# Two heads on separate 64-row halves of TensorE in both score passes of a segment-wise attention block

## The chip, the cores and the metric

The kernel runs on one core of one Trainium2 chip. The metric is the device time of one execution in microseconds (us), and lower is better. The kernel before takes 1942.58 us, the median of three runs (1942.33, 1942.58 and 1944.91).

## The reference

`block` computes one transformer block on 2048 tokens of width 576: a modulated layer norm, an attention with 32 heads of 18 features, a second modulated layer norm and a gated feed-forward of width 4608. The attention works on four segments of 512 tokens. Inside a segment it is an ordinary causal softmax, and a running memory of earlier segments is added. Cut to the part that the change touches:

```python
for s in range(4):
    qs, ks, vs = q[:, :, s], k[:, :, s], v[:, :, s]
    logits = einsum("bhqd,bhkd->bhqk", qs, ks) * scale + mask
    p = softmax(logits, axis=-1)
    a_dot = einsum("bhqk,bhkd->bhqd", p, vs)
    o = g * (phi(qs) @ M) / (phi(qs) @ z) + (1 - g) * a_dot
    M, z = M + phi(ks).T @ vs, z + phi(ks).sum()
```

Everything is float32. To keep enough digits, q and k are split into a high and a low part of TensorE's fp32r type, so that one head's dot product of 18 features becomes one of 54 rows (high by high, high by low, low by high).

## The kernel before

The kernel has three stages. Stage one (up to about 258 us) normalises, projects q, k and v (line 93, tiles `pp` and `pv`) and builds the memory matrices. Its order is made by a scheduler. Stage two (258 to about 617 us) is the attention of all heads. Its order is written out by hand. Stage three is the feed-forward (lines 1090 and 1152), which the change does not touch.

**Units.** The attention is cut into 32 units: a segment and a group of four heads. For each unit `load_stack` (L151) brings k and q into two stacks, `kst` and `qst`. Two heads, called e = 0 and e = 1, form a pair, and a unit has two pairs, a = 0 and a = 1. In `kst` a pair's heads lie one below the other: rows 0 to 53 hold e = 0, rows 54 to 107 hold e = 1. In `qst` each of the four heads has its own column block with its 54 rows filled and the other head's 54 rows zero (L117, L118 write the zeros once for each of the stack buffers). A product over all 108 rows therefore gives one head's scores, because the zero rows cancel the other head.

**First pass** (`p1_step`, L164): queries stand still and keys stream. Its only purpose is each query's largest score. It has four steps i = 3, 2, 1, 0 with n = 512, 384, 256, 128 keys. TensorE writes the scores into a PSUM bank (tag `s1`, two buffers), and VectorE adds the mask and takes the maximum (L179, tile `junk`). The maxima go through GpSimd, a transpose (L193, `pmt`), a ScalarE copy and a DMA to `mD`, and `load_m` (L160) brings them back as two further rows, 108 and 109, of `qst`. Rows 108 and 109 of `kst` are ones (L119).

**Second pass** (`p2_step`, L565): keys stand still and queries stream, over 110 rows, so that the maximum is subtracted inside the product. Its steps are j = 0 to 3 with n = 512, 384, 256, 128 queries. TensorE writes into a bank with tag `s2` (two buffers), ScalarE takes the exponential (L579, tile `Pt`) and GpSimd zeroes the upper triangle (L583). For n up to 256 one product streams two heads, and one exponential takes 512 columns.

**Order.** The loop at L1168 runs unit u's second pass beside unit u+2's first pass. Each is a generator that yields after each PSUM bank: four banks for n = 512, four for n = 384, two for n = 256, one for n = 128, eleven in all. In each of the eleven steps the loop issues one bank of the second pass, one bank of the first pass, and then the events that the string `PAT[...][k]` lists. Events with TensorE work are `V` (L596, probabilities by values, four heads on four 32-column tiles of the array), `m` (the transpose of the maxima), `c` (L617, transposes of the result), `A` (L765, the memory's part), `R` and `Z` (transposes of a finished segment) and `M` (L694, the output projection of the segment before, from unit 9 on). The event `n` sends the maxima out and issues `load_m`. Engines take their instructions in the order in which they were issued, so a product that waits for a bank holds up what stands behind it on TensorE.

The first passes of units 0 and 1 lie in stage one (`early`, L243), a bank at a time between the projections.

## Time and profile before

| what | value |
|---|---|
| median of three runs | 1942.58 us |
| span of the profiled execution | 1946.8 us |
| TensorE busy over the span | 1901.2 us, 98% |
| VectorE busy | 1533.1 us, 79% |
| ScalarE busy | 824.8 us, 42% |
| GpSimd busy | 1020.6 us, 52% |
| granted TensorE clock, mean | 0.993 |
| first product of the second pass of unit 0 / unit 31 | 260.34 us / 609.05 us |

The profiled execution is one more execution, with the hardware profiler on. Its span is 4.2 us longer than the median of the runs. All durations come from it. A busy TensorE is not a TensorE at its peak: the record of a product holds its whole way through the array, and the next product starts before it ends. What a product costs in a stream is the distance from its start to the start of the next one. In such a listing a row is one or several equal instructions: start, length, engine, line, operation, output and inputs, shape and count. PEld is the load of the operand that stands still ("weights"), which can run while the product before is under way.

### The profile page before, as it was taken

Reading aid. Unit: us, or ns where it says so; the run is one execution under the profiler, and the core shown is the slowest. Engines: PE = TensorE matmul, PEld = TensorE weight load, DVE = VectorE, ACT = ScalarE, POOL = GpSimd, SP = SyncE. Lnnn points to the kernel's source line nnn. Section 1 sums busy time; section 2 is a strip of 40 time slices with the busy share of each in tenths; the row PEclk is TensorE's granted clock in tenths of the full one; section 3 lists DMA queues with packets and bytes.
Section 4 is the critical chain, followed back from the end, with each engine's and each line's share of the span. In section 5 each row is a group of like instructions: output and inputs, shape, how many; then the busy total and the mean of one; then the engine's idle time right before and its main releaser. Section 6 shows DMA issues by size and latency. Waiting matters only on the chain.

```text
span 1946.8 us, 31901 instructions
## 1 busy us (share of the span) xinstructions
PE 1901.2 (98%) x11119; PEld 1593.1 (82%) x11119; DVE 1533.1 (79%) x3218; ACT 824.8 (42%) x1652; POOL 1020.6 (52%) x1396
## 2 busy tenths in 40 slices
PE   7999999999999899999999999999999999999999
PEld 4887865676766678888888888888888888888888
DVE  6575257878786999898898988979888888878886
ACT  2222256767667434344344343433333333333332
POOL 5322235455544866556565565556565564655551
PEclk9999999999999899999999999999999999999999
DMA  7776564444443332232222222174211211112111
GB/s 207 244 227 233 203 204 140 131 139 150 136 128 125 92 135 101 89 106 80 80 106 83 82 84 78 60 264 146 74 62 45 74 62 59 60 62 74 62 57 50
DMA packets 114354, 223.59 MB, mean 115 GB/s; under 512 B 22992, under 2 KB 40784, under 8 KB 112720
## 3 DMA queue, kind: packets, MB, share of 16 engines
q1 hardware_dynamic: 111936, 215.61, 34.2%
q0 software_dynamic: 576, 5.11, 0.7%
q8 instruction: 88, 1.44, 0.3%
q10 hardware_dynamic: 1680, 0.82, 0.2%
q14 instruction: 74, 0.61, 0.1%
HBM read 161.11 MB, written 60.36 MB: 114 GB/s over the span
## 4 chain that ended last, share of the span: by engine, by line
PE 88%; DVE 4%; DMA 4%; ACT 1%; issue 1%; POOL 1%; SPq 1%; POOLq 0%; ACTq 0%; DVEq 0%
PE M L1090 39%; PE pd L1152 23%; PE pp L93 4%; PE s L576 4%; PE av L596 4%; PE s L174 4%; PE pv L93 3%; PE pw L694 2%; DMA O<-in_wgu_dram 1%; DMA mD<-mr 1%; PE pn L765 1%; PE pm L429 1%; PE px L617 1%; PE pr L346 1%; DVE y L923 1%
## 5 line engine op out<-in xcount | busy, mean ns | idle before, releaser
L1090 PE MATMUL M<-y,wh 128*128 128x512 f32 x2520 | 792.0, 393 | 5.0 <-DVE cu L1106 2.1
L1090 PEld LDWEIGHTS M<-y,wh 128*128 128x128 f32 x2520 | 473.7, 188 | 101.7 <-issue 3.9
L1067 POOL TENSOR_TENSOR wh<-O,wh 32x128 fp32r<-32x128 f32 x504 | 296.6, 593 | 423.0 <-ACT wh L1065 271.3
L1090 PE MATMUL M<-y,wl 128*128 128x512 f32 x1008 | 394.7, 392 | 0.0
L1059 POOL TENSOR_TENSOR O<-O 128x384 f32<-128x384 f32 x288 | 315.4, 1095 | 75.0 <-DMA O<-in_wgu_dram 42.9
L1152 PE MATMUL pd<-dh,ah 128*128 128x288 f32 x1152 | 340.3, 295 | 0.2 <-DVE acc L1155 0.2
L1152 PE MATMUL pd<-dl,ah 128*128 128x288 f32 x1152 | 340.3, 295 | 0.0
L1152 PE MATMUL pd<-dh,al 128*128 128x288 f32 x1152 | 340.1, 295 | 0.0
L1110 ACT CAST ah<-sg 128x512 fp32r<-128x512 f32 x144 | 89.5, 621 | 547.8 <-DVE sg L1107 422.0
L1155 DVE TENSOR_TENSOR acc<-acc,pd 128x576 f32<-128x576 f32 x288 | 216.5, 752 | 111.8 <-PE pd L1152 108.4
L1066 DVE TENSOR_TENSOR wl<-O,wh 128x256 fp32r<-128x256 f32 x504 | 286.2, 568 | 6.0 <-ACT wh L1065 5.2
L179 DVE CUSTOM_DVE_ANT_0 junk<-s,tri 128x256 bf16<-128x256 f32 (+3 forms) x512 | 228.7, 487 | 77.2 <-PE s L174 69.8
L1065 ACT CAST wh<-O 128x384 fp32r<-128x384 f32 x504 | 242.8, 507 | 0.0
L1152 PEld LDWEIGHTS pd<-dl,ah 128*128 128x128 f32 x1152 | 217.4, 189 | 11.8
L1152 PEld LDWEIGHTS pd<-dh,ah 128*128 128x128 f32 x1152 | 216.7, 188 | 11.6 <-DVE acc L1155 0.6
L579 ACT ACTIVATE Pt<-s 128x512 f32<-128x512 f32 (+1 forms) x352 | 186.5, 559 | 88.1 <-PE s L576 72.0
L1152 PEld LDWEIGHTS pd<-dh,al 128*128 128x128 f32 x1152 | 216.6, 188 | 0.0
L1090 PEld LDWEIGHTS M<-y,wl 128*128 128x128 f32 x1008 | 190.0, 188 | 29.6
L1102 ACT ACTIVATE sg<-sg 128x512 f32<-128x512 f32 x144 | 91.2, 633 | 222.7 <-DVE sg L1101 222.7
L576 PE MATMUL s<-qs,ks 110*128 110x512 f32 (+2 forms) x384 | 150.5, 409 | 5.7 <-DMA qs<-mD 4.4
L174 PE MATMUL s<-ks,qs 108*128 108x256 f32 (+3 forms) x512 | 141.2, 327 | 3.3 <-DMA ks<-kD 1.4
L583 POOL TENSOR_SCALAR_AFFINE_SELECT Pt<-Pt 128x512 f32<-128x512 f32 x128 | 81.6, 648 | 100.6 <-ACT Pt L579 100.2
(428 smaller groups left out, 2836.6 us busy)
## 6 DMA issues: line engine op xcount, KB each, us to landing
O<-in_wgu_dram SPq DMA_DIRECT2D x72, 768.0 KB
ks<-kD SPq DMA_DIRECT2D x68, 216.0 KB
qs<-qD SPq DMA_DIRECT2D x68, 216.0 KB
kD<-fh SPq DMA_DIRECT2D x16, 512.0 KB
qD<-fh SPq DMA_DIRECT2D x16, 512.0 KB
yD<-st SPq DMA_DIRECT2D x28, 256.0 KB
y<-yD SPq DMA_DIRECT2D x7, 1024.0 KB
wml<-in_w_mod_dram SPq DMA_DIRECT2D x24, 216.0 KB
```

The source lines that it names most:

```text
L93: nc.tensor.matmul(ps, lhsT=a, rhs=b, start=(k == 0), stop=(k == 13))
L174: nc.tensor.matmul(bank[:, n * (h - h0):n * (h - h0) + n], lhsT=qst[b][0:108, h, 128 * i:128 * i + 128], rhs=kst[b][0:108, h // 2, 0:n], s ...
L179: nc.vector.tensor_tensor_reduce(junk[:, :n], bank[:, n * (h - h0):n * (h - h0) + n], tri[:, L - n:], 1.0, -3e38, op0=ALU.add, op1=ALU.max ...
L576: nc.tensor.matmul(bank[:, n * (g - h):n * (g - h + w)].rearrange("p (a b) -> p a b", a=w), lhsT=kst[u % NB][0:110, g // 2, 128 * j:128 * ...
L579: nc.scalar.activation(pt[:, h:h + per, :n], bank[:, :n * per].rearrange("p (a b) -> p a b", a=per), AF.Exp, scale=SCALE)
L1059: nc.gpsimd.tensor_tensor(o[:, d], o[:, a], o[:, b], op=op)
L1065: nc.scalar.copy(wh, o)
L1066: later.append(lambda: nc.vector.tensor_tensor(wl, o[:, 0:2], f32(wh[:, 0:2]), op=ALU.subtract))
L1067: later.append(lambda: nc.gpsimd.tensor_tensor(wh[32:64, 2], o[32:64, 2], f32(wh[32:64, 2]), op=ALU.subtract))
L1090: nc.tensor.matmul(bank, lhsT=a, rhs=b, start=(n == 0), stop=(n == 6))
L1152: nc.tensor.matmul(pd[:, h, :288], lhsT=a[:, tk], rhs=w[:, f, sl], start=(k == 0), stop=(k == 5))
L1155: nc.vector.tensor_tensor(o, o, pd[:, :, :288], op=ALU.add)
```

## The change

Each head of a pair now has its own half of the array. Head e = 0 uses rows 0 to 53 (and 54, 55 for the maxima and ones), head e = 1 uses rows 64 to 117 (and 118, 119), in both stacks. `qst` shrinks from four column blocks to two, and the zeros and their memsets are gone. Each product is over 54 or 56 rows and is issued for a tile of 64 by 128 cells, at row 0 or row 64, where it was issued for the whole 128 by 128 array. In each step the second pass takes heads of one half and the first pass heads of the other half, and the next step swaps them. For n = 256 and n = 128 the two products of a bank are now the two heads with the same e. For n = 128 a unit has two banks where it had one, so both passes have twelve steps, and the event strings are spread over twelve. The rows of ones and the maxima are loaded by two DMAs where one did it.

```diff
     def new_stack(b, stk):
-        qst[b] = stk.tile([P, 4, L], F32R, tag=f"qs{b}", name=f"qs{b}")
+        qst[b] = stk.tile([P, 2, L], F32R, tag=f"qs{b}", name=f"qs{b}")
         kst[b] = stk.tile([P, 2, L], F32R, tag=f"ks{b}", name=f"ks{b}")
-        nc.vector.memset(f32(qst[b][:, 0:2]), 0.0)
-        nc.gpsimd.memset(f32(qst[b][:, 2:4]), 0.0)
-        nc.sync.dma_start(f32(kst[b][108:110]).rearrange("p a (b c) -> p (a b) c", c=P),
-                          ones[0:2, :].unsqueeze(1).to_broadcast([2, 8, P]))
+        for e in range(2):
+            nc.sync.dma_start(f32(kst[b][64 * e + 54:64 * e + 56]).rearrange("p a (b c) -> p (a b) c", c=P),
+                              ones[0:2, :].unsqueeze(1).to_broadcast([2, 8, P]))
...
     # p1_step
-        per = L // n if n <= 256 else 1
-        for h0 in range(0, 4, per):
+        groups = [((0, 1),), ((0, 0),), ((1, 1),), ((1, 0),)] if n > 256 else [((0, 1), (1, 1)), ((0, 0), (1, 0))]
+        for g, hs in enumerate(groups):
...
-                                 lhsT=qst[b][0:108, h, 128 * i:128 * i + 128],
-                                 rhs=kst[b][0:108, h // 2, 0:n], start=True, stop=True)
+                r = slice(64 * e, 64 * e + 54)
+                nc.tensor.matmul(bank[:, n * x:n * x + n], lhsT=qst[b][r, a, 128 * i:128 * i + 128],
+                                 rhs=kst[b][r, a, 0:n], start=True, stop=True)
...
     # p2_step
+        groups = [((0, 0),), ((0, 1),), ((1, 0),), ((1, 1),)] if n > 256 else [((0, 0), (1, 0)), ((0, 1), (1, 1))]
...
-                                 lhsT=kst[u % NB][0:110, g // 2, 128 * j:128 * j + 128],
-                                 rhs=qst[u % NB][0:110, g:g + w, 128 * j:L], start=True, stop=True)
+                r = slice(64 * e, 64 * e + 56)
+                nc.tensor.matmul(bank[:, n * x:n * x + n], lhsT=kst[u % NB][r, a, 128 * j:128 * j + 128],
+                                 rhs=qst[u % NB][r, a, 128 * j:L], start=True, stop=True)
...
-            for k in range(11):
+            for k in range(12):
```

34 lines of the change are left out of this document (17 added, 17 removed), and 6 rows, old and new, of the table PAT.

## The prediction

> **What bounds the kernel now.** I read the page first: the span and the chain of work that ended last.
>
> ```profile
> span 1946.8 us, 31901 instructions
> PE 88%; DVE 4%; DMA 4%; ACT 1%; issue 1%; POOL 1%; SPq 1%; POOLq 0%; ACTq 0%; DVEq 0%
> ```
>
> TensorE carries 88% of the chain, so shorter score passes can pay, if the stretches in which they lie are themselves held by TensorE. So next come the busy times by stage.
>
> ```profile
> 93.00:118.00 25.00, 24.11 (x114) 18.20 (x113) 23.93 (x68) 5.78 (x11) 5.74 (x9) 1.00 0.63 210
> 118.00:165.00 47.00, 47.00 (x300) 41.46 (x299) 28.76 (x71) 13.41 (x25) 10.72 (x16) 1.00 0.73 245
> 258.00:380.00 122.00, 113.70 (x778) 71.55 (x778) 92.93 (x383) 88.37 (x181) 63.17 (x114) 0.97 0.48 142
> 380.00:620.00 240.00, 239.58 (x1799) 166.91 (x1797) 183.93 (x770) 167.32 (x336) 118.83 (x246) 1.00 0.44 131
> ```
>
> Columns after the length: TensorE, its weight loads, VectorE, ScalarE, GpSimd, granted clock. The first passes of units 0 and 1 lie between 93 and 165 us: up to 118 us VectorE is as full (23.93 of 25) as TensorE, after that TensorE alone is. The attention has two parts. From 380 us (units 11 on) TensorE is never free (239.58 of 240) while VectorE has 77% and ScalarE 70%. Before 380 us TensorE has pauses (113.70 of 122), though neither VectorE nor ScalarE is fuller. The chain of waits says what fills them:
>
> ```profile
> 254.28 9.62 DMA qs<-qD
> 298.22 5.61 DMA mD<-mr
> 303.90 1.80 DMA qs<-mD
> ...
> 291.79 1.83 DMA qs<-mD
> ...
> 326.88 1.87 DMA qs<-mD
> ```
>
> The second is the round trip of a unit's maxima through DRAM: 5.61 + 1.80 = 7.4 us, and it ends when the next unit's second pass can begin. The last two rows are the ends of the same trip in two more units. In all of them a faster TensorE waits for the DMA.
>
> **What the change removes: every second score product's time.** The prices, start to start, are in the timeline of one unit; one product of 512 columns, of 384, of 256 and of 128 (with a weight load each):
>
> ```profile
> 589.78 0.50 PE L576 MATMUL s<-qs,ks 110*128 110x512 f32 x1
> 590.12 0.40 PE L174 MATMUL s<-ks,qs 108*128 108x512 f32 x1
> 590.35 0.40 PE L576 MATMUL s<-qs,ks 110*128 110x512 f32 x1
> 590.59 0.39 PE L174 MATMUL s<-ks,qs 108*128 108x512 f32 x1
> 590.90 0.42 PE L596 MATMUL av<-Pt,vq 128*32 128x256 f32 x4
> ...
> 594.78 0.34 PE L576 MATMUL s<-qs,ks 110*128 110x384 f32 x1
> 594.95 0.34 PE L174 MATMUL s<-ks,qs 108*128 108x384 f32 x1
> 595.13 0.34 PE L576 MATMUL s<-qs,ks 110*128 110x384 f32 x1
> ...
> 598.43 0.50 PE L576 MATMUL s<-qs,ks 110*128 110x512 f32 x1
> 598.77 0.40 PE L174 MATMUL s<-ks,qs 108*128 108x256 f32 x2
> 599.01 0.40 PE L576 MATMUL s<-qs,ks 110*128 110x256 f32 x2
> 599.25 0.56 PE L174 MATMUL s<-ks,qs 108*128 108x128 f32 x4
> ...
> 599.13 0.53 PEld L174 LDWEIGHTS s<-ks,qs 108*128 108x128 f32 x4
> ```
>
> A product of 512 takes 0.23 us (590.12, 590.35, 590.59), of 384 takes 0.175, of 256 takes 0.12 (two from 598.77 to 599.01). Four of 128 are set by their weights: four loads last 0.53, one 0.19 (the common length), so (0.53 - 0.19)/3 = 0.11 each.
>
> If the two halves work side by side, a step costs one half's products. Steps of 512: 0.46 becomes 0.23, four of them save 0.93. Steps of 384: 0.35 becomes 0.175, four save 0.70. Steps of 256: 0.23 + 2 x 0.12 = 0.47 becomes 0.24, two save 0.47. The one step of 128 (2 x 0.12 + 0.11 x 3 + 0.06, about 0.63) becomes two steps of 2 x 0.11, saving 0.19. That is 2.3 us for each unit with both passes, 30 of them: 69 us. Whether halves overlap is not in this trace. Its nearest row is the four column tiles of line 596:
>
> ```profile
> 597.44 1.07 PE L596 MATMUL av<-Pt,vq 128*32 128x512 f32 x8
> ...
> 589.00 0.16 PEld L596 LDWEIGHTS av<-Pt,vq 128*32 128x32 f32 x8
> ```
>
> Eight records of 512 columns are over after 598.43 - 597.44 = 0.99 us, four tiles at a time; one after another at 0.23 they would need 1.8. The eight weight loads of another such step are over in 0.16. I take full overlap, and keep none as the other end. The Trainium skill, "TensorE: Matmul & The Clock Gate", Part 3 (measured speedup), gives 3.07 times for four row tiles of 32 rows at 512 columns; no run here shows it, and by it the saving for two halves would also be nearly whole.
>
> **What it adds: changes of the array's tiling.** Stage one has one place where products for a 64-row tile stand among full ones.
>
> ```profile
> 53.35 0.40 PE L93 MATMUL pp<-hr,wqkh 128*128 128x512 f32 x1
> 53.58 0.40 PE L93 MATMUL pp<-hr,wqkl 128*128 128x512 f32 x1
> 53.91 0.46 PE L416 MATMUL ptk<-ident,pf 64*128 64x64 f32 x4
> 54.30 0.50 PE L93 MATMUL pp<-hh,wqkh 128*128 128x512 f32 x1
> 54.64 0.40 PE L93 MATMUL pp<-hh,wqkl 128*128 128x512 f32 x1
> ...
> L416 PE MATMUL ptk<-ident,pf x60: 222/272/421, 39.0 to 189.1; 128*128 128x128 f32 x48, 64*128 64x64 f32 x12
> ```
>
> Into the tile: 53.58 to 53.91 is 0.33 where 0.23 is usual, so 0.10. After such a change the weights can't be loaded ahead, as the first score product after line 596 shows (589.78 to 590.12, 0.34 instead of 0.23): 0.11 more. Out of it: the group's last product is 0.22 long, so it starts at 53.91 + 0.46 - 0.22 = 54.15, the next at 54.30, which is 0.15 where products this short stand 0.06 apart (0.24 for three distances, the first with 0.11 for weights): 0.09; and then again unloaded weights, 54.30 to 54.64, 0.11. So 0.20 in and 0.20 out.
>
> How often, I counted in the built programs' order of TensorE's instructions. Beside a `V` nothing is new, since line 596 (128x32 tiles) changes the tiling already before. New are the visits next to `M`, `c`, `A` and `R`. Units 0 to 8 (no `M` yet): 18 in, 17 out, 7 us. Units 9 to 31: 99 in, 93 out, 38 us. Stage one, where one bank of a first pass stands alone between projections and so has no partner: 22 and 22, 9 us.
>
> **How much of it reaches the end.** Units 9 to 31: 21 x 2.3 - 38 = 10 us less TensorE time; TensorE is full there, but the exponentials bound some steps:
>
> ```profile
> PEld s L576 <- ACT Pt L579: 37.2, 64, 0.8
> ```
>
> TensorE's weight loads wait 64 times for ScalarE to free a bank. I take 85%: 8.5 us faster. Units 0 to 8: 9 x 2.3 - 7 = 14 us less; the maxima's round trip does not shrink, only the steps before it, so I take 40%: 5.5 us faster (bounds 0 and 14). Stage one: half of the visits lie before 118 us, where VectorE hides part: 7 of 9 us slower. Then SP's queue at the start of the attention:
>
> ```profile
> 249.72 1.49 SPq L119 DMA_DIRECT2D ks<-ones  x2
> 254.28 0.90 SPq L158 DMA_DIRECT2D qs<-qD  x1
> ```
>
> Two DMAs of ones become four, 0.75 each, ahead of unit 2's loads, whose last (254.28, landing 9.62 later) ends the wait of the first score product of unit 2: 1.5 us slower, on the path. The second `load_m` DMA costs at most one more issue of a few tenths, only in the few units that wait for the maxima: under 1 us, I take 0. The dropped memsets (GpSimd, VectorE) run under the projections and give 0 (with that cover gone, a microsecond each). 32 more exponentials: two of 256 columns for one of 512 on an engine that is 30% free, 0. The shorter last step frees VectorE earlier, which `m` may use, 0.
>
> Sum: -8.5 - 5.5 + 7 + 1.5 = -5.5 us against the profiled span, 1946.8 to 1941.3. The median of the runs is 4.2 below that span, so I put the same difference there: 1942.6 - 5.5, about **1937 us**.
>
> **The rivals.**
>
> 1. *Slower: the halves don't really overlap.* Place: every step; price: the changes of tiling (7 + 38 + 9) and 1.5 stay, 55 us, against a saving that shrinks. With none of it, nine tenths of the 55 us show, as TensorE is not quite full everywhere: 1942.6 + 50 = 1993. It decides at 55/69: below four fifths of full overlap the kernel is slower. A halfway form: products overlap but the two halves' weights load one after the other, 0.11 each. Then steps of 384 save 0.53 in all, of 256 0.06, of 128 lose 0.25, and each of some eight entries per unit costs 0.11 more: 0.93 + 0.53 + 0.06 - 0.25 - 0.9 = 0.4 per unit, 12 us against 55, about 1981. Against both: line 596's four column tiles and their loads run side by side. For: no row of before has two row tiles at once. 10% and 14%.
> 2. *Products start strictly in the order of issue.* In a step of 256 or 128 a bank's two products share a half, and the partner's come behind, so only the middle two overlap: three slots of 0.12 or 0.11 instead of two. That takes 4 slots, 0.46 us, from each of 30 units, 14 us, some 11 at the end: 1948. The Trainium skill has this as a rule in "TensorE: Matmul & The Clock Gate", Part 3 (what overlaps and what doesn't). Line 596's rows do not show the issue order of its passes, so the trace leaves it open. 8%.
> 3. *The other engines set the pace.* The order was cut for eleven steps, VectorE needs 184 of 240 us in bursts, and the maxima's round trip ends more units. The saving stays small, the switches in stage one are whole: 1942.6 + 1.5 + 7 - 6, about 1945. For it: the 64 waits above. 13%.
> 4. *More than I take.* Both parts of the attention turn TensorE's relief into time, 10 + 14, and a tenth of the 45 us of tiling changes there hides behind the waits for banks: 1942.6 - 24 - 4.5 + 8.5, about 1922. For it: the 64 waits for banks, which are there already; against it: the maxima's round trip. 10%.
>
> **How the numbers follow.** My forecast, 1928 to 1946, has 45%. The range leaves out the case without overlap and the far end of the fourth: 1918 to 1985. A measurement of this kernel can tell about 0.2%, 3.9 us, from no change: 1938.7 to 1946.5 is "same". Faster: most of the forecast (34%) and the fourth rival, 44%. Same: 10% of the forecast, 6% of the third, 2% of the second, 18%. Slower: the first rival's 24%, 6% of the second, 7% of the third, and 1% left, 38%.
>
> **What would show it.** Right: in the timeline of a unit, a product of L576's successor and the first pass's product start within hundredths of each other, 0.11 + 0.23 later the next; entries and exits of 0.2; units after 380 us shorter by about 0.4; stage one longer by 7. Wrong: partners 0.23 apart (first rival), weight loads of partners 0.11 apart (its halfway form), partners of 256 waiting for the second of the bank before (second), TensorE pauses ended by VectorE or ScalarE (third).

## The result and the profile after

The changed kernel takes **1974.26 us** (median of four runs, 1971.58 to 1975.89), the kernel before beside it 1942.45 us. The ratio is 1.0156, with a 95% interval of 1.0142 to 1.0171: 1.6% slower. The forecast was 1937, faster. The time lies inside the range of 1918 to 1985, but the likeliest case and its sign were wrong.

The page of the changed kernel, first its span, then the chain of work that ended last by engine:

```profile
span 1974.2 us, 32222 instructions
PE 88%; DMA 4%; DVE 4%; ACT 2%; issue 1%; SPq 1%; POOL 1%; DVEq 0%; ACTq 0%; POOLq 0%
```

The chain says nothing new: TensorE carries 88% as before. What moved is seen by stage. The attention is cut at the first product of units 0, 9 and 31 in each kernel. The columns after the length are TensorE, its weight loads, VectorE, ScalarE, GpSimd (busy us and count), then the granted clock, the share of DMA and GB/s. First the kernel before (units 0 to 8, units 9 to 30):

```profile
260.30:359.80 99.50, 91.20 (x614) 55.13 (x612) 76.70 (x319) 72.32 (x149) 54.15 (x97) 0.97 0.49 146
359.80:609.00 249.20, 249.15 (x1858) 174.32 (x1854) 197.86 (x827) 175.31 (x353) 122.77 (x255) 1.00 0.43 130
```

Then the changed kernel:

```profile
268.30:381.00 112.70, 102.52 (x649) 51.91 (x649) 76.87 (x317) 74.63 (x156) 53.94 (x97) 0.76 0.44 128
381.00:637.20 256.20, 252.44 (x1946) 146.55 (x1944) 198.79 (x830) 178.66 (x375) 123.82 (x255) 1.00 0.44 128
```

Three places lose. Stage one ends at 268.3 instead of 260.3 (+8). Units 0 to 8 take 112.7 instead of 99.5 (+13), and their clock column reads 0.76 instead of 0.97: TensorE ran at half clock for about half of that time. Units 9 to 30 take 256.2 instead of 249.2 (+7) at an undisturbed clock. The rest gives back 0.8, and the sum is the 27.4 us between the two spans. The medians are 31.8 apart, because the profiled execution of the kernel before was 4.4 us longer than its median run and that of the changed kernel was not; so some 4 us of the loss are in no row here.

Yet the overlap is there. This is the end of one unit and the start of the next (unit 24) in the changed kernel, TensorE only; each row is start, length, engine, line:

```profile
556.48 0.39 PE L578 MATMUL s<-qs,ks 56*128 56x256 f32 x1
556.49 0.38 PE L175 MATMUL s<-ks,qs 54*128 54x256 f32 x1
556.71 0.28 PE L578 MATMUL s<-qs,ks 56*128 56x256 f32 x1
556.71 0.28 PE L175 MATMUL s<-ks,qs 54*128 54x256 f32 x1
...
560.29 0.64 PE L598 MATMUL av<-Pt,vq 128*32 128x256 f32 x8
560.86 0.50 PE L578 MATMUL s<-qs,ks 56*128 56x512 f32 x1
560.86 0.50 PE L175 MATMUL s<-ks,qs 54*128 54x512 f32 x1
561.29 0.43 PE L598 MATMUL av<-Pt,vq 128*32 128x128 f32 x8
561.65 0.28 PE L194 MATMUL pmt<-ident,mc 128*32 128x128 f32 x1
561.86 0.50 PE L578 MATMUL s<-qs,ks 56*128 56x512 f32 x1
```

Partners start within 0.01 us. A step of 512 between two V events (560.86 to 561.29) takes 0.43. The same steps before:

```profile
534.16 0.50 PE L576 MATMUL s<-qs,ks 110*128 110x512 f32 x1
...
535.28 0.64 PE L596 MATMUL av<-Pt,vq 128*32 128x256 f32 x8
535.86 0.50 PE L576 MATMUL s<-qs,ks 110*128 110x512 f32 x1
536.20 0.40 PE L174 MATMUL s<-ks,qs 108*128 108x512 f32 x1
536.53 0.43 PE L596 MATMUL av<-Pt,vq 128*32 128x128 f32 x8
536.88 0.28 PE L193 MATMUL pmt<-ident,mc 128*32 128x128 f32 x1
536.92 0.48 PE L576 MATMUL s<-qs,ks 110*128 110x512 f32 x1
```

There the step takes 536.53 - 535.86 = 0.67. So 0.24 is saved on it, where 0.23 was priced. Note the last two rows of both fences too: from the small transpose `pmt` to the next score product it was 0.04, now it is 0.21.

### The profile page after: what moved, and what is told of

Read it like the earlier page. It is cut to its first block, busy times and chain, and to the rows that moved or that the text cites. A ratio compares the mean times of both kernels' runs of the same rounds, so it can differ in the third digit from the quotient of the medians.

```text
span 1974.2 us, 32222 instructions
## 1 busy us (share of the span) xinstructions
PE 1922.1 (97%) x11247; PEld 1559.8 (79%) x11247; DVE 1521.0 (77%) x3214; ACT 830.9 (42%) x1684; POOL 1015.4 (51%) x1392
## 4 chain that ended last, share of the span: by engine, by line
PE 88%; DMA 4%; DVE 4%; ACT 2%; issue 1%; SPq 1%; POOL 1%; DVEq 0%; ACTq 0%; POOLq 0%
PE M L1092 40%; PE pd L1154 23%; PE s L578 5%; PE pp L93 5%; PE av L598 4%; PE pw L696 3%; PE pv L93 2%; PE s L175 2%; DMA mD<-mr 1%; DVE y L925 1%; PE pm L430 1%; PE px L619 1%; ACT Pt L581 1%; PE pn L767 1%; DMA qs<-mD 1%
## 5 line engine op out<-in xcount | busy, mean ns | idle before, releaser
L1068 DVE TENSOR_TENSOR wl<-O,wh 128x256 fp32r<-128x256 f32 x504 | 274.7, 546 | 5.9 <-ACT wh L1067 5.1
L581 ACT ACTIVATE Pt<-s 128x512 f32<-128x512 f32 (+2 forms) x384 | 192.1, 526 | 109.4 <-PE s L175 81.5
L175 PE MATMUL s<-ks,qs 54*128 54x256 f32 (+3 forms) x512 | 167.9, 399 | 5.7 <-DMA qs<-qD 4.1
L578 PE MATMUL s<-qs,ks 56*128 56x256 f32 (+3 forms) x512 | 161.0, 393 | 8.2 <-ACT Pt L581 4.3
L578 PEld LDWEIGHTS s<-qs,ks 56*128 56x128 f32 x512 | 84.9, 199 | 101.8 <-ACT Pt L581 63.1
## 6 DMA issues: line engine op xcount, KB each, us to landing
yD<-st SPq DMA_DIRECT2D x28, 256.0 KB
```

Source lines behind the costliest of these rows:

```text
L175: nc.tensor.matmul(bank[:, n * x:n * x + n], lhsT=qst[b][r, a, 128 * i:128 * i + 128], rhs=kst[b][r, a, 0:n], start=True, stop=True)
L578: nc.tensor.matmul(bank[:, n * x:n * x + n], lhsT=kst[u % NB][r, a, 128 * j:128 * j + 128], rhs=qst[u % NB][r, a, 128 * j:L], start=True, ...
L581: nc.scalar.activation(pt[:, h:h + 2 * w - 1:2, :n], bank[:, :n * w].rearrange("p (a b) -> p a b", a=w), AF.Exp, scale=SCALE)
L1068: later.append(lambda: nc.vector.tensor_tensor(wl, o[:, 0:2], f32(wh[:, 0:2]), op=ALU.subtract))
```

## The experiments

For the place of each gain or loss I use the starts of the records. The table gives the first product of unit 0, the length of units 0 to 8 and 9 to 30, what follows the first product of unit 31, and the time at half clock that the trace records within units 0 to 8.

| kernel | unit 0 at | units 0-8 | units 9-30 | rest | half clock |
|---|---|---|---|---|---|
| before | 260.3 | 99.5 | 249.2 | 1337.7 | 6.8 |
| after | 268.3 | 112.8 | 256.2 | 1336.9 | 54.6 |
| attention_only | 260.3 | 111.0 | 256.0 | 1336.4 | 47.8 |
| late_only | 255.2 | 97.8 | 262.1 | 1339.0 | 3.4 |
| order_only | 261.8 | 102.0 | 256.3 | 1336.5 | 6.8 |
| same_half | 269.7 | 121.8 | 279.5 | 1339.6 | 71.7 |
| before_light | 258.8 | 98.1 | 249.2 | 1337.1 | 10.2 |
| after_light | 265.2 | 109.3 | 255.6 | 1337.9 | 51.2 |
| after_group | 263.6 | 115.8 | 259.3 | 1339.2 | 61.4 |
| after_fill | 267.3 | 125.4 | 258.0 | 1337.9 | 37.5 |
| after_pad | 264.1 | 112.5 | 264.7 | 1338.1 | 44.4 |
| pick | 259.3 | 105.7 | 252.2 | 1338.6 | 23.9 |
| before_n | 258.8 | 99.9 | 249.8 | 1337.9 | 6.8 |
| pick2 | 265.8 | 103.5 | 251.2 | 1337.4 | 10.2 |
| pick3 | 283.8 | 106.9 | 249.3 | 1337.6 | 10.2 |
| pick3_all | 285.0 | 105.7 | 250.7 | 1338.1 | 13.7 |

A second table splits units 11 to 29 (19 units without the ends) by kind: each TensorE product counted from its start to the start of the next, summed in us.

| kernel | score products | V | all others | sum |
|---|---|---|---|---|
| before | 111.4 | 51.5 | 55.9 | 218.9 |
| order_only | 117.7 | 51.5 | 55.7 | 224.9 |
| after | 91.8 | 52.6 | 79.0 | 223.4 |
| same_half | 113.7 | 51.9 | 78.6 | 244.2 |
| after_light | 90.6 | 53.0 | 80.1 | 223.8 |
| after_group | 100.0 | 52.8 | 73.0 | 225.7 |

Each row is one execution. The row of `after_light` holds 10.2 us at half clock, that of `after_group` 3.4; the other four have none.

My first theory was: three separate losses, of which the last is saving that is lost in waits for banks. Its rivals: one loss that drags the others along, or an overlap that is worth less than counted.

### Do the three stages add up?

`attention_only` keeps the first passes of units 0 and 1 in stage one on the whole array. It is the kernel before up to there; against it, the stacks are then loaded again as halves, and the attention uses the changed kernel's passes (`p1_half`, `p2_half`; `U0` is 0):

```diff
             for u in range(2):
-                load_stack(u, u)
+                load_stack(u, u, True)
                 load_m(u, u)
...
-                yield from p1_step(u, u % NB, 3 - i, ps, wk, 4)
+                yield from (p1_half if u >= U0 else p1_step)(u, u % NB, 3 - i, ps, wk, 4)
```

> The first passes of units 0 and 1 (stage one) stay on the whole array; all units of the attention use the halves, with the twelve-step order. Theory (three stages add up: stage one +8, units 0 to 8 +13, units 9 to 30 +7, with the granted clock at half speed as the cause in units 0 to 8): about 1966 us, first product of the second pass of unit 0 back near 260.3, and still some 50 us at half clock between 260 and 390 us. Rival (what happens at the start of the attention is a late consequence of stage one, whose loads and maxima come later): the half clock mostly goes as well, about 1953 us.

Measured: 1968.25 us, ratio 1.0121 (1.0106 to 1.0136). Unit 0 starts at 260.3 again, and units 0 to 30 are nearly as slow as in the changed kernel. The eight microseconds of stage one are separate, and the theory holds. How far a single trace can tell them: the five kernels with the old stage one reach unit 0 at 255.2 to 260.3 (before, attention_only, late_only, before_light, before_n), the six with halves there at 263.6 to 269.7, so 258.7 against 266.4 on the mean.

`late_only` uses halves only for units 11 and later (`U0 = 11`):

```diff
-            ga = chain(*[p2_step(u, j) for j in range(4)])
+            ga = chain(*[(p2_half if u >= U0 else p2_step)(u, j) for j in range(4)])
...
-                yield from p1_step(u, u % NB, 3 - i, ps, wk, 4)
+                yield from (p1_half if u >= U0 else p1_step)(u, u % NB, 3 - i, ps, wk, 4)
```

> Units 0 to 10 stay as before; units 11 to 31 use the halves (so the loop's passes 9 and 10 have one half-row pass each, and from 11 on both). Theory (units from 9 on lose by themselves: changes of tiling paid in full, saving lost in waits for banks): about 1948 us, 0.2 to 0.35 us more per unit after 400 us, clock 1.00 and no further half-clock stretch. Rival (the late units lose only because the early ones left them late or out of step): about 1935 us, as my sum had it.

Measured: 1958.87 us, 1.0079 (1.0053 to 1.0104). That is 11 us more than I wrote, and 7 of them are of the experiment's own making: the loop's passes 9 and 10, where one pass is on halves and has no partner, take 14.3 and 14.6 us instead of 10.7 and 11.1. Units 11 to 30 take 233.2 us as in the changed kernel, against 227.4. So the late units lose by themselves, at clock 1.00.

### Are the readers of the banks the bound?

Both kernels with readers of half the length, so that half of the scores enter neither a maximum nor an exponential:

```diff
-                nc.vector.tensor_tensor_reduce(junk[:, :n], bank[:, n * x:n * x + n], tri[:, L - n:],
+                m = n // 2 if 2 <= u else n
+                nc.vector.tensor_tensor_reduce(junk[:, :m], bank[:, n * x:n * x + m], (tri[:, 0:m] if m < n else tri[:, L - n:]),
...
-            nc.scalar.activation(pt[:, h:h + 2 * w - 1:2, :n], bank[:, :n * w].rearrange("p (a b) -> p a b", a=w),
-                                 AF.Exp, scale=SCALE)
+            m = n // 2 if u >= 1 else n
+            nc.scalar.activation(pt[:, h:h + 2 * w - 1:2, :m], bank[:, :n * w].rearrange("p (a b) -> p a b", a=w)[:, :, :m],
+                                 AF.Exp, scale=0.02 * SCALE)
```

> The kernel before with lighter readers: VectorE's maxima (from unit 2) read only half of a bank's columns, and the exponential (from unit 1) only half, with a smaller scale, so the result is not the attention any more; TensorE's work is unchanged. Control for the next. Theory (TensorE alone sets the pace after 380 us): units 9 to 30 shorten by little, from 249.2 us to 243 to 249; whole about 1935 to 1942.

> The changed kernel with the same lighter readers (maxima and exponentials over half of the columns). Theory (the saving of the halves is lost in waits for banks that VectorE and ScalarE have not emptied): with readers at half length units 9 to 30 take 8 to 12 us less than the same units of the light kernel before, and TensorE's weight loads no longer wait for ScalarE (38 us of waits fall under 10). Rival (the halves themselves save less than I counted, or changes of tiling cost more): units 9 to 30 stay 4 to 8 us longer than those of the light kernel before, whatever the readers do. In units 0 to 8 the half clock stays or grows by the clock theory, since TensorE idles no less.

Measured: 1941.06 (0.9984, 0.9973 to 0.9995) and 1967.92 (1.0118, 1.0095 to 1.0140). Units 9 to 30 of the two, the light kernel before first:

```profile
357.00:606.20 249.20, 248.13 (x1858) 174.73 (x1855) 147.80 (x823) 133.13 (x352) 122.82 (x254) 1.00 0.44 130
```

```profile
374.50:630.10 255.60, 251.54 (x1946) 144.89 (x1943) 146.04 (x827) 136.61 (x375) 123.17 (x254) 0.98 0.45 129
```

VectorE and ScalarE fall by a quarter (198 to 148 and 175 to 133 us in the kernel before), and the stage keeps its 249.2 and nearly its 256.2. Part of the second is the clock: the light changed kernel had 10.2 us at half clock in unit 12 (its column reads 0.98). In units 14 to 29, at full clock, it takes 183.4 us against 187.0 in the changed kernel; the two kernels before take 182.8 (light) and 183.7. So lighter readers give 3.6 us there, 3.0 of them in score products, about what the changed kernel had lost in these units; but with them the halves still gain nothing over the light kernel before, where I had expected 8 to 12 us over units 9 to 30. My theory falls in this form: neither engine's load sets the pace. That the length of a single read counts is shown below. The many weight loads said to wait for ScalarE are no evidence either. Those rows count the idle time of the load queue, which runs beside the products; with light readers they were no fewer (38 instead of 33 in the kernel before, 90 instead of 75 in the changed one, from 391 to 610 us).

### Order, overlap and changes of tiling apart

`order_only` has the twelve steps and the new grouping, but all products on the whole array with the old stacks:

```diff
-                r = slice(64 * e, 64 * e + 54)
-                nc.tensor.matmul(bank[:, n * x:n * x + n], lhsT=qst[b][r, a, 128 * i:128 * i + 128],
-                                 rhs=kst[b][r, a, 0:n], start=True, stop=True)
+                nc.tensor.matmul(bank[:, n * x:n * x + n], lhsT=qst[b][0:108, 2 * a + e, 128 * i:128 * i + 128],
+                                 rhs=kst[b][0:108, a, 0:n], start=True, stop=True)
```

`same_half` is the changed kernel with its overlap within a step taken away:

```diff
-        groups = [((0, 1),), ((0, 0),), ((1, 1),), ((1, 0),)] if n > 256 else [((0, 1), (1, 1)), ((0, 0), (1, 0))]
+        groups = [((0, 0),), ((0, 1),), ((1, 0),), ((1, 1),)] if n > 256 else [((0, 0), (1, 0)), ((0, 1), (1, 1))]
```

> The kernel before with the changed kernel's order alone: twelve steps, its grouping of heads in the banks, two banks for n = 128; all products on the whole array, stacks as before. Theory (the halves and their changes of tiling make the loss, not the order): 1942 to 1947 us, units 9 to 30 within 2 us of 249.2. Rival (the twelve steps and the exponentials that they add set the pace): units 9 to 30 at 254 to 257, as in the changed kernel, about 1952.

> The changed kernel, but in each step both passes take the head of the same half, so that nothing overlaps and all changes of tiling stay. Theory (the overlap is worth nearly its full 2.3 us per unit where no bank is waited for, and is eaten by changes of tiling): units 9 to 30 cost 1.4 to 2.3 us more each than in the changed kernel, 30 to 50 us over the 22, so 287 to 306 us against 256.2; the whole 2010 to 2040. Rival (the overlap is worth little, because the engines that read the banks set the pace): units 9 to 30 under 275 us, whole under 2000.

Measured: `order_only` 1957.49 (1.0069, 1.0051 to 1.0087), `same_half` 2011.84 (1.0343, 1.0301 to 1.0385). Both surprised me. On the whole array the new grouping alone costs 7 us in units 9 to 30, as much as the whole change: the 128-column steps have eight products, each set by its weight load of 0.11 (0.88), where there were six and 0.63; that is 0.25 of the 0.32 us that a unit lost. Halves run those products in pairs, so this is not a cost that the changed kernel still has in full; but it shows that it gains no time over its own order there (256.2 against 256.3). And taking the overlap away costs 23 us in these units, 1.1 each, where I had counted 2.3. The second table says where: score products go from 113.7 to 91.8. That is a lower bound of the overlap's worth, because with both passes on one half products of the next step, on the other half, still run beside this one: in all 17 places of units 9 to 30 where two steps of 384 follow each other, their second-pass products start within 0.01 us.

The same table gives the price of the changes of tiling in place: everything that is neither score nor V goes from 55.9 to 79.0 (23.1 us in 19 units), the same in `same_half`.

`after_group` puts the M events together in twos, which takes away 72 of the changes in units 9 to 31:

```diff
-PAT = (["", "V2", "V3 E m D", "M0", "n M1 Q G", "c", "M2 d", "V0 g", "h A0 q M3 R S X", ...
+PAT = (["", "V2", "V3 E m D", "", "n Q G", "M0 M1 c", "d", "V0 g", "h A0 q M2 M3 R S X", ...
```

> The changed kernel with its M events put together in twos, next to another event on the whole array or next to a V event where possible. In units 9 to 31 this takes away 45 of 93 changes from the halves to the whole array and 27 of 99 back; work and score passes are the same. Theory (each change costs 0.2 us and they are the main part of what ate the saving): 72 x 0.2 = 14 us less, units 9 to 30 at 241 to 246 instead of 256.2. Rival (these units are held by waits for banks or by the maxima, so fewer changes only lengthen other waits): units 9 to 30 at 252 to 258.

Measured: 1975.25 us, 1.0169 (1.0151 to 1.0187); units 9 to 30 at 259.3, not at 241 to 246. That is the rival's side, and 1 us above its range; unit 25 alone came out 1.8 longer than in the changed kernel, with 3.4 us at half clock. In units 11 to 29 the other products fell by 6.0 us, but the score products rose by 8.2: with nothing between them, score steps wait. The groups of what TensorE waited for in units 9 to 30, first the changed kernel, then this one (time, times, longest); the kernel before has no such row there:

```profile
PE s L578 <- ACT Pt L581: 1.6, 8, 0.3
PE s L175 <- DVE mx L180: 0.9, 3, 0.3
```

```profile
PE s L578 <- ACT Pt L581: 5.3, 18, 0.5
PE s L175 <- DVE mx L180: 2.3, 6, 0.5
```

What they wait for is a bank's round trip, not a busy reader: the time from the product that fills a bank to the end of the read that empties it. The start of unit 24 in the changed kernel, with the reader:

```profile
558.79 0.32 PE L578 MATMUL s<-qs,ks 56*128 56x128 f32 x1
...
558.95 0.27 PE L578 MATMUL s<-qs,ks 56*128 56x128 f32 x1
...
559.07 0.45 PE L578 MATMUL s<-qs,ks 56*128 56x512 f32 x1
...
559.26 0.38 ACT L581 ACTIVATE Pt<-s 128x256 f32<-128x256 f32 x1 [0.77 <-PE s L175]
...
559.70 0.50 PE L578 MATMUL s<-qs,ks 56*128 56x512 f32 x1 [0.18 <-ACT Pt L581]
```

The products of 558.79 and 558.95 fill one of the two `s2` banks, the one of 559.07 the other. ScalarE was idle for 0.77, reads the first bank from 559.26 to 559.64, and only then can the third step start, at 559.70. Two steps of 512 side by side last from 559.06 to 560.29, 1.23 us; before they lasted 534.16 to 535.28, 1.12. With two banks a step can start no sooner than one product, one handover and one read after the step before last, some 0.75 us here. At 0.46 a step nobody noticed; at 0.28 (558.79 to 559.07) it is the bound. In units 11 to 29 there are 14 places where two steps of 512 follow each other. The second-pass products start 0.34 apart in 3 of them and 0.61 to 0.76 in 11; before they were 0.54 to 0.58 apart, and with the light readers mostly 0.52. So a shorter read shortens the trip. No run gave a pass a third bank, which would have tested it directly.

### Halves only where no change of tiling is added

`pick` keeps the eleven steps and the whole array, and takes halves only for the first steps of a unit:

```diff
+SPL = ((0, 1, 2), (0, 1, 2), (0, 1, 2), (0, 1))
...
+                half[0] = SFROM <= u < STO and k in SPL[q // 4 * 2 + u % 2]
...
+                r = slice(64 * (h % 2), 64 * (h % 2) + 54) if half[0] else slice(0, 118)
```

> The eleven-step order of before, the whole array nearly everywhere, and separate halves only in those first steps (n = 512, the first three steps of a unit, or two in the odd units of a segment's second half) whose neighbours are V events, so that no change of tiling is added; one M0 and one A1 are moved by one place for that; the other half's rows are zero, and the old maxima are cleared by two more small DMAs per unit. Theory (the saving is real, 0.23 us a step, and only the added changes of tiling eat it): units 9 to 29 shorter by 0.3 to 0.65 us each, 6 to 13 us in all, granted clock as before in units 9 on; the whole 1925 to 1940, the first nine units open (0 to -5, or up to +10 if the clock falls there). Rival (VectorE and ScalarE, who empty the banks, set the pace): units 9 to 29 within 2 us of before, the whole 1942 or more.

Measured: 1954.65, 1.0060 (1.0043 to 1.0077), not 1925 to 1940. Seven of units 13 to 24 came out 0.4 to 0.6 us shorter; five units were 1.2 to 2.8 us longer. In units 9 to 30 TensorE waited 6.0 us for the maxima, up to 2.3 at a time, and the clock was at half for 10.2.

`before_n` (control) sends the maxima one step earlier, and `pick2` has that, halves from unit 9 on and one clearing DMA less:

```diff
-PAT = (["", "V2", "V3 E m D", "M0", "n M1 Q G", ...
+PAT = (["", "V2", "V3 E m D", "M0 n", "M1 Q G", ...
...
-SFROM, STO = 0, 30
+SFROM, STO = 9, 30
...
-            for a in range(0, 4, 2):
-                nc.sync.dma_start(f32(qst[b][54:56, a]).rearrange("p (b c) -> p b c", c=P),
-                                  tri[0:2, :P].unsqueeze(1).to_broadcast([2, 4, P]))
+            nc.sync.dma_start(f32(qst[b][54:56, 0:4:2]), zD)
```

> The kernel before with one edit: the event that sends a unit's maxima out and issues their load stands one step earlier in three of the four unit types. Control for the next kernel. TensorE sets the pace from unit 9 on, so those units stay within 2 us of 249.2 in all; the first nine may gain up to 5 us, since they wait for that round trip. Whole 1936 to 1943.

> As the last version with halves in the first steps only, but from unit 9 on only, with the maxima sent one step earlier, the old maxima cleared by one DMA instead of two, and the rows of ones written by memsets instead of DMAs. Theory (in that version the maxima's round trip took over as the bound in the units that came out long; without it the units keep their 0.45 to 0.55 us): units 9 to 29 take 6 to 12 us less than those of the kernel with the earlier maxima alone; the whole 1925 to 1936. Rival (the second maxima DMA, 0.65 us of issue, still sets the pace): several units again 1 to 3 us long, the whole 1938 or more.

Measured: 1947.66 (1.0014, 1.0004 to 1.0023) and 1958.51 (1.0067, 1.0051 to 1.0084): no gain. The maxima still came late in five units (4.8 us). `pick3` loads them by one DMA, `pick3_all` is the same with halves from unit 0:

```diff
-        for e in range(2):
-            nc.sync.dma_start(f32(qst[b][64 * e + 54:64 * e + 56, e:4:2]), v[e])
+        nc.sync.dma_start(f32(qst[b][62:66]).rearrange("p a t -> p (a t)"),
+                          m_dram(u).rearrange("e r -> (e r)")[0:8192].rearrange("(p t) -> p t", p=4))
```

> Halves in the first steps only (n = 512, next to V events), from unit 9 on, with the maxima and ones of both halves in rows 62 to 65, so that one DMA loads a unit's maxima as in the kernel before (they are written by two); products over all 64 or 128 rows, unused rows zero; maxima sent one step earlier. Theory (in the last version of this kind only the later landing of the second maxima DMA held the units): waits for the maxima fall from 9.7 us to under 4, units 9 to 29 take 6 to 11 us less than the 240.7 of before, the whole 1930 to 1940. Rival (the maxima's round trip is too long for shorter units however it is loaded): several units again 0.5 to 2 us over before, the whole 1943 or more.

> The same with halves in the first steps of all units from 0 to 29. Theory (with all rows in use the clock stays up, so the first nine units gain nothing or a little): units 0 to 8 within 3 us of the same kernel without them, whole within 4 us of it. Rival (the shorter steps lower the clock there whatever the rows): units 0 to 8 longer by 5 us or more, half clock of 15 us or more between 260 and 380 us.

Measured: 1979.81 (1.0188, 1.0173 to 1.0204) and 1974.65 (1.0164, 1.0138 to 1.0190). The 23 us of late start are my own: the DMAs that fill the new maxima buffers with zeros lie in stage one. Units 9 to 30 are at 249.3, within 0.1 of before. Four units without any wait, 13 to 16, take 11.40 + 11.88 + 11.42 + 11.06 = 45.8 us against 47.8 before, so 0.5 each; units 11, 12 and 19 lose 3.9, with three waits for the maxima of 3.2 us in all and 3.4 us at half clock. So the saving exists where no change of tiling is added and no bank is waited for, and then the maxima's round trip takes over. In units 0 to 8 `pick3_all` is no longer than `pick3` (105.7 against 106.9) and has 13.7 us at half clock against 10.2, as its theory had it; both are longer than the kernel before there (99.5), and I did not look for the reason. No version that I ran with the whole computation beats the kernel before.

### Why the clock falls

Each window is 3.41 us, the step in which the clock changed in all traces. The kernel before, at the start of its attention, then the changed kernel:

```profile
264.50:267.91 3.41, 3.33 (x12) 2.02 (x10) 3.10 (x10) 2.33 (x5) 0.64 (x1) 0.73 0.95 344
267.91:271.33 3.42, 3.34 (x18) 1.46 (x16) 1.69 (x7) 3.19 (x7) 1.67 (x3) 0.77 0.71 237
271.33:274.74 3.41, 3.41 (x26) 1.85 (x27) 2.54 (x16) 1.58 (x3) 3.00 (x7) 1.00 0.48 148
```

```profile
274.74:278.15 3.41, 3.41 (x11) 2.55 (x10) 2.77 (x11) 2.42 (x5) 0.64 (x1) 0.50 0.67 273
...
281.56:284.98 3.42, 3.17 (x20) 1.64 (x18) 1.75 (x12) 1.24 (x4) 1.22 (x2) 0.50 0.22 64
```

Both fall when TensorE waits for the first loads; the kernel before is back after 3.4 us, which lie across the first two windows, the changed kernel after 23.9, though TensorE's column is full. The Trainium skill ("TensorE: Matmul & The Clock Gate", Part 1) says that the clock falls after one or more idle windows of about 3.4 us and comes back after one or more busy windows. The window's length agrees; that a window or two in which TensorE's column is full would be enough does not, by these rows.

`after_fill` adds 14 products of 288 columns in each of units 0 to 8, where the M events are:

```diff
+            if n == "M" and w < 0:
+                for _ in range(14 * int(a) // WC, 14 * (int(a) + 1) // WC):
+                    nc.tensor.matmul(wps[0][:, :288], lhsT=fz[:, :P], rhs=fz, start=True, stop=True)
```

> The changed kernel with 14 more products of 288 columns on the whole array in each of units 0 to 8, into a bank that is free there, where the output projection's products stand in the later units; nobody reads them. Theory (in units 0 to 8 the shorter score passes leave TensorE so little work per window that the clock is halved): with more work the clock stays at 1.00 for most of 268 to 390 us and the nine units take 100 to 108 us, less than the 112.8 of the changed kernel although they do more. Rival (the clock falls for another reason, or is a consequence and not the cause of the long units): half clock as before, and the nine units take 118 to 130 us.

Measured: 1986.43 (1.0218, 1.0203 to 1.0233); units 0 to 8 take 125.4 us. Wrong: half clock went down only from 54.6 to 37.5, and the units grew by the added work. `after_pad` fills the rows of each half up to 64 with zero rows:

```diff
-                r = slice(64 * e, 64 * e + 54)
+                r = slice(64 * e, 64 * e + 64)
...
-                r = slice(64 * e, 64 * e + 56)
+                r = slice(64 * e, 64 * e + 64)
```

> The changed kernel with every score product over the full 64 rows of its half; the added rows are zero (stacks zeroed once, and the old maxima cleared by two more small DMAs per unit). Same products, same times of a product, same order. Theory (the clock gate counts the rows that take part, and in units 0 to 8 the 54 or 56 rows of a half keep TensorE's activity under its threshold): half clock between 268 and 390 us falls from 54.6 us to under 20, and units 0 to 8 from 112.8 to 98 to 105 us; the whole 1958 to 1967. Rival (short steps and waits lower the activity, not the rows): half clock stays above 40 us, units 0 to 8 at 109 to 115, the whole 1972 to 1978.

Measured: 1980.24 (1.0182, 1.0161 to 1.0203), half clock 44.4, units 0 to 8 at 112.5. Here the rival was right: more rows alone don't bring it back. (The 8 us more in units 9 to 30 lie in four units, with 17 us at half clock.)

Three benches, each executed once, measured the clock by itself; they hold no attention. The groups of the first, for pairs (`read` is the ScalarE copy that the next group waits for):

```diff
+    def pair(n, k):
+        for _ in range(n):
+            for _ in range(k):
+                nc.tensor.matmul(b0, lhsT=w[0:56], rhs=a[0:56], start=True, stop=True)
+                nc.tensor.matmul(b1, lhsT=w[64:120], rhs=a[64:120], start=True, stop=True)
+            read(b1)
```

> No attention at all: streams of 512-column products with random data, each stretch followed by 70 products on the whole array. First 150 products on one half alone without a pause, 150 pairs on both halves without a pause; then groups of 1, 2, 4 or 8 products (or pairs) after each of which TensorE waits for ScalarE to copy the bank, once on the whole array, once as pairs, and for 1 and 4 on one half. The result is just a copy of the input. Theory (the clock gate counts how much of the array works, so half-filled or shorter work lets the clock fall): one half alone without pause falls to 0.5, pairs stay at 1.0, and in the groups the pairs fall earlier than the whole array. Rival (it counts only the time in which TensorE works, whatever part of it): one half alone without pause stays at 1.0, and whole array, pairs and one half fall at the same group size.

> Second bench of the clock, again no attention and the input copied as result: groups of products, a wait for ScalarE after each group: 4 on the whole array; 4 pairs with 64 rows each; 4 of 112 rows and 4 of 96 rows on the whole array; 3 on the whole array; 5 pairs of 56 rows; 8 and 16 on one half of 56 rows; then one per wait on the whole array, and 4 per wait right behind it. Theory (the gate counts array rows at work times time, with a threshold between 6.4 and 6.6 whole-array products of 512 columns per 3.41 us): 4 pairs with 64 rows keep 1.0; 4 of 112 rows (about 6.3) fall or sit on the edge, 4 of 96 rows (5.4) fall, 3 on the whole array (about 5.8) fall, 5 pairs (7) keep 1.0, 8 on one half (4.3) fall, 16 on one half (5.4) fall. Rival (it counts products or busy time by tile, not rows): 4 of 112 and of 96 rows on the whole array keep 1.0 like 128 rows, and 8 and 16 on one half keep it too.

> Third bench of the clock, no attention, the input copied as result. Ahead of each stretch 14 products with a wait each bring the clock down to half; then comes a stretch with no wait at all, and the question is how soon it is back: 90 pairs of 56 rows; 90 products on the whole array; 90 on one half; 30 times a pair of 512 and two whole-array products of 288 (two changes of tiling each time); 30 times the same four products all on the whole array; 30 times a pair of 56 rows and four column tiles as in the V events; 30 times the same on the whole array; 30 times a pair of 64 rows and four column tiles. Theory (half-filled rows and changes of tiling count as too little work, which is why the attention stayed at half clock for 24 us with TensorE busy throughout): the whole-array stretches are back within 7 us, those that mix pairs and whole array or column tiles stay at half clock for 10 us or more, and one half alone stays so to the end. Rival (any stretch without waits brings the clock back, so that the waits of the attention keep it down): all eight are back within 7 us.

In the first bench, one half alone without a wait, begun at full clock; four products on the whole array for each wait; four pairs of 56 rows:

```profile
23.00:57.20 34.20, 34.20 (x151) 27.52 (x150) 0.00 (x0) 0.00 (x0) 0.00 (x0) 1.00 0.43 139
432.90:466.50 33.60, 21.20 (x73) 12.15 (x72) 0.00 (x0) 9.96 (x17) 0.00 (x0) 1.00 0.00 0
482.40:526.60 44.20, 38.66 (x145) 22.02 (x144) 0.00 (x0) 9.96 (x17) 0.00 (x0) 0.64 0.00 0
```

In the second, four pairs of 64 rows; four products of 112 rows; and again four products on the whole array for each wait, but begun at half clock:

```profile
71.90:105.90 34.00, 27.32 (x146) 15.18 (x144) 0.00 (x0) 9.96 (x17) 0.00 (x0) 1.00 0.00 1
122.00:168.00 46.00, 33.58 (x73) 19.07 (x72) 0.00 (x0) 9.97 (x17) 0.00 (x0) 0.57 0.00 0
540.00:626.20 86.20, 63.88 (x124) 36.17 (x125) 0.00 (x0) 17.67 (x31) 0.00 (x0) 0.50 0.00 0
```

In the third, without any wait but after a stretch at half clock: 90 products on one half; 30 times a pair and two whole-array products; the same on the whole array; pairs and column tiles as in the V events:

```profile
106.67:145.00 38.33, 38.33 (x91) 29.36 (x90) 0.00 (x0) 0.58 (x1) 0.00 (x0) 0.50 0.00 0
165.19:209.60 44.41, 44.41 (x120) 23.22 (x120) 0.00 (x0) 0.58 (x1) 0.00 (x0) 0.50 0.00 0
229.58:253.00 23.42, 23.42 (x119) 20.43 (x118) 0.00 (x0) 0.59 (x1) 0.00 (x0) 0.90 0.00 1
272.00:315.50 43.50, 43.50 (x301) 10.57 (x300) 0.00 (x0) 0.58 (x1) 0.00 (x0) 0.97 0.00 1
```

Rows count: at the same rhythm 128 rows, or 2 x 64, hold the clock, and 112, or 2 x 56, lose it. The guess of a threshold at 6.4 products was off: three on the whole array for each wait, which I put under it, held 1.00, and five pairs of 56 rows, which I put over it, fell (0.74 on the mean). Where a stretch begins counts too: the same groups of four products held 1.00 for 34 us when they began at full clock and stayed at 0.50 for 86 us when they began at half. In the third bench my theory was half right. A stream of pairs and whole-array products, busy all the time, never came back from half clock in 44 us, one half alone not in 38 (begun at full clock, in the first bench, the same stream kept 1.00 for 34 us); but pairs mixed with column tiles were back in one window, which I had put among those that stay.

One number orders all of this. For each window I added up the time in which operands stream (a column of a score product 0.43 ns at full clock, of a V product 1.0, of a transpose 0.84, from the distances between starts; twice that at half clock) times the share of rows in use. This is an estimate from the records. In three benches and both kernels the clock fell only after windows with a share of 0.43 or less, nearly always under 0.40, and came back only after windows with 0.73 or more, nearly always over 0.80. Neither edge is sharp: three products for each wait held 1.00 at 0.39, and in the changed kernel some windows of 0.72 to 0.79 left the clock at half. The stream of pairs and whole-array products has 0.55 to 0.61, one half alone 0.45, pairs with column tiles 0.78 to 0.85. In units 0 to 8 at full clock the kernel before has 0.64 on the mean, the changed kernel 0.48; at half clock the changed kernel has 0.66. So it lives close to the falling edge and, once fallen, often does too little per window to come back. Padding gave 0.50 and 0.65, filling 0.56 and 0.69: both in the right direction, neither enough. In units 9 on the share goes from 0.76 to 0.59, and the clock holds in both; in three variants of the changed kernel it fell there as well (after_group 3.4 us, after_light 10.2, after_pad 17.1).

## Why the prediction was wrong

**Overlap of the halves: right.** Partners start within 0.01 us and load their weights side by side (the loads of 556.48 and 556.49 last 0.18 each). Both forms of the first rival are out, though its 1981 came nearest to the result, by a mechanism that isn't there.

**Start order: right.** The second rival is out: the first pass's product of 556.49 started before the second pass's product of 556.71, which was issued ahead of it. The rule of the Trainium skill behind that rival ("TensorE: Matmul & The Clock Gate", Part 3) does not hold across row tiles in this trace. Nor does the sentence ahead of the prediction that engines take their instructions in the order of issue, as far as TensorE's two halves go.

**Stage one and the start: right.** +7 was forecast, +8 measured (7.7 on the mean of the kernels above). The 1.5 us for two more DMAs of ones can be seen in unit 0, where the wait for the first loads grew; the waits of the score products, before and after:

```profile
PE s L174 <- DMA ks<-kD: 1.4, 1, 1.4
PE s L174 <- DMA qs<-qD: 1.2, 1, 1.2
```

```profile
PE s L175 <- DMA qs<-qD: 4.1, 1, 4.1
```

That is 2.6 against 4.1. That the two DMAs make the difference was not tested.

**Units 0 to 8: wrong, -5.5 forecast, +13.3 measured.** The failed step is "9 x 2.3 - 7 = 14 us less", of which I took 40%. It took the clock of the stretch (0.97) as given. A faster TensorE that still waits for the maxima's round trip does less work per window, and the clock halved for 54.6 us instead of 6.8. That the fall goes with the work per window is shown by the benches; that the whole 13 us come from it isn't shown, since no version brought the clock fully back. The waits at the start (1.5 us) and the order (`order_only` lost 2.5 us there) may be part of it; no run separates them.

**Units 9 to 31: wrong, -8.5 forecast, +7 measured.** For units 11 to 29 my prices gave 19 x 2.3 = 43.7 less and about 160 changes x 0.2 = 32 more, a gain of 12; measured was a loss of 4.5. Two terms of the step "21 x 2.3 - 38 = 10 us less TensorE time" were mis-sized. First, the changes on the side of the other products: half of 32 is 16, the table shows 23.1. My entry of 0.10 came from a product of 512 columns ahead of the change. Behind products of 128 or 152 columns the next one used to start much sooner, and now it waits the same 0.2. In units 11 to 29 there are 65 such places (`pmt`, `px`, `pto`, `ptr`, `pn`): the median distance to the next score product was 0.03 to 0.04 and is 0.20 to 0.22. Behind the 39 M groups (288 columns) it was 0.13 and is 0.22. Together that is 15.5 us; the distances from an M product to the next one that isn't a score product give 6.8 more. Here are the four transposes of a finished unit, before:

```profile
529.21 0.60 PE L617 MATMUL px<-ident,avs 128*128 128x128 f32 x4
529.57 0.42 PE L576 MATMUL s<-qs,ks 110*128 110x384 f32 x1
```

and after:

```profile
554.35 0.60 PE L619 MATMUL px<-ident,avs 128*128 128x128 f32 x4
554.87 0.44 PE L578 MATMUL s<-qs,ks 56*128 56x384 f32 x1
```

From the first transpose to the score product it was 0.36 and is 0.52. Among the 65 places are the 19 `pmt` transposes, 0.17 each, which I hadn't counted as changes at all. Second, the score products: 43.7 less the other 16 would be 28, measured 19.6. Most of the missing 8 stand in ten places where a step of 128 and two steps of 512 follow each other: they take 1.51 each, where my prices give 0.8 to 0.9 (0.22 + 0.46, and the first weights and the change behind them). The rows of 558.79 to 559.70 show a bank's round trip in such a place; that it makes all of the 8 is not shown. I had looked for waits for ScalarE and taken 85%, but the row I took for evidence counts the idle time of the load queue and not TensorE's; the limit that the rows point to, two banks and steps as short as 0.28, stood in no row of before, and `after_group` made it visible.

**The other rivals.** The third ("the other engines set the pace") was right in sign and near in place, but its reason, that the other engines set the pace, does not hold: a quarter less load gave 3.6 us in units 14 to 29, by shorter reads of single banks. The fourth is out. None of my cases had the clock in it.

Still open: how much of units 0 to 8 would be left at a steady clock.

## What to carry to other kernels

Before you price a cheaper product, look at what stands around it: a step between two events of another tiling costs two changes of some 0.2 us here, and a step with nothing around it can't come sooner than its bank's round trip; only steps beside events that change the tiling anyway keep the saving. Read waits for banks on the rows of the products, not on those of the weight loads. And in a stretch where TensorE waits for something else, taking work away from it can cost the clock, so work out the share of a window that it streams before and after.

## What the hardware did that I had not expected

In these traces the clock has two edges with a wide gap: it fell after a window of 3.41 us with a share of work, counted in rows, under about 0.4, and came back after one over about 0.75 to 0.8 (my estimate above). So a stream without a single wait can stay at half clock for long: one half alone for 38 us, pairs mixed with whole-array products for 44 us. And products on separate halves can start out of the order of issue: the one of 556.49 stood behind the one of 556.71.
